# Two of sixteen head pairs of a hash attention: keys and queries grouped by two hash bits, products inside the four groups alone

## The chip, the cores and the metric

The kernel runs on one core of a Trainium2 chip. The metric is the device time of one execution in microseconds. Five engines work side by side, each through its own list of instructions in order: TensorE (PE; its weight loads are PEld), VectorE (DVE), ScalarE (ACT), GpSimd (POOL) and SyncE (SP), which does nothing but issue DMAs. An instruction that waits holds up everything behind it on its engine.

## The reference, cut to what matters

```python
batch, n_heads, seq, head_dim = (4, 8, 768, 64)
...
q_bits = (np.einsum('bhsd,dk->bhsk', q, proj) > 0)     # 6 bits
k_bits = (np.einsum('bhsd,dk->bhsk', k, proj) > 0)
...
mask = q_bucket[:, :, :, None] == k_bucket[:, :, None, :]
scores = np.where(mask, scale * np.matmul(q, k.transpose(0, 1, 3, 2)), -1e9)
...
attn = np.exp(scores - max)
out = np.matmul(attn / (attn.sum(-1) + 1e-9), v)
...
xt = x.transpose(0, 2, 1)                    # x: (B, S, 512), the heads side by side
u = x + (np.maximum(xt @ w_tok1, 0.0) @ w_tok2).transpose(0, 2, 1)
return u + np.maximum(u @ w_ch1, 0.0) @ w_ch2
```

A query sees only the keys whose six hash bits are all its own. What follows the attention is a token mixer (over the 768 positions) and a channel mixer (over the 512 channels).

## The kernel before

There are 32 heads of 768 tokens and 64 channels. Two heads of one batch are a **pair**, so there are 16 pairs, four to a batch, and the function `attention` walks through them in the loop over `n` at L560. A pair's 768 queries are two halves of 384; its 768 keys are six blocks of 128.

For each pair the loop does this, on engines that overlap from pair to pair:

- `scores` (L459): for each half and block a matmul of hash bits (bf16, L476) and two of channels (f32, L476 too) are summed in one pair of PSUM banks, so that a key of another bucket gets a large negative score. Each matmul uses 32 of the array's 128 rows, and four of them run side by side. ScalarE takes the exponential of each block (L388). PSUM has four pairs of banks, tag `sc`, handed out in turn, which scores, sums, hashes and weighted values all share.
- `Half.add` and `add_last` (L420, L430): VectorE sums the six blocks of exponentials of a half, five operations of 128x768 each half (L424, L428, L432).
- `Quotients.sums` (L503): TensorE sums over the keys with a matrix of ones (L509); ScalarE makes a first reciprocal as exp(-ln) (L513, L514); `newton` (L517) improves it on VectorE (L522, L524) and ScalarE spreads it (L530); `divide` (L532, L534) puts quotients into `XT`, the attention's result with channels on the partitions. The sums, `newton` and `divide` of a pair run during the pair after it.
- `Hash(n + 1)` (L317): TensorE projects the next pair's queries and keys (L325, L330), VectorE makes bits of them (L342, L343) into a scratch place in `XT`, and DMAs spread them to the rows of `bits` (`spread`, L335): eight from SP for keys (L350) and eight from POOL for queries (L353).
- `Half.weigh` (L434): TensorE multiplies exponentials and values (L443), ScalarE moves the result out (L453).
- `Conversion` (L133): the weights come as float64 and are turned to float32 in 12 chunks, one a pair in pairs 0 to 11: one ScalarE operation (L169), four on VectorE in `join` (L179 to L188) and one in `end` (L198).
- `bounce` (L220): after every second pair two pairs' results are transposed on VectorE in 32x32 blocks (L225) and written to DRAM (`bounced`, L230), from where `fetch` (L235, L237) brings a batch in token order into `x0` or `x1` for the mixer. The fetch of batch 0 into `x0` stands in pair 8.

After pair 15 the pools of the attention are given back, and the token mixer (L742 and L782) begins with batch 0, then the channel mixer (L869). The mixer's first matmul takes a PSUM bank that the attention's last `newton` has read.

All of it is written out by hand in the order in which each engine is to run it; no scheduler moves anything. DMAs of SP run through one queue in the order of issue. At its end the kernel looks whether any score was too large for the way in which exponentials are taken here (`excess`); if so a careful version runs everything again.

## Time and profile before

| | us |
|---|---|
| three runs | 780.22, 781.08, 781.44 (median 781.08) |
| the profiled execution | 779.55, its span 777.8 |
| attention in it, first scores to the mixer's first matmul | 5.84 to 301.93 |
| busy in the span: PE, PEld, DVE, ACT, POOL | 770.8, 513.0, 677.6, 453.5, 115.4 |

Times below are counted from the start of the span. A row of the chain of waits, in order of time, has the start, the length, and the engine, tile and line of a piece of the chain. A row of the timeline has the start, the time from the first to the last end of merged instructions, engine, line, operation, output and input with their shapes, and how many there are; in brackets stands how long the engine sat idle before it, and for whom. A row of groups has the busy time and the mean of one in ns behind the bar. A row of windows has the busy time of each engine in a stretch, the granted TensorE clock, the busy share of the DMA engines and GB/s.

### The profile page before, as it was taken

Reading aid. Unit: us, or ns where it says so; the run is one execution under the profiler, and the core shown is the slowest. Engines: PE = TensorE matmul, PEld = TensorE weight load, DVE = VectorE, ACT = ScalarE, POOL = GpSimd, SP = SyncE. Lnnn points to the kernel's source line nnn. Section 1 sums busy time; section 2 is a strip of 40 time slices with the busy share of each in tenths; the row PEclk is TensorE's granted clock in tenths of the full one; section 3 lists DMA queues with packets and bytes.
Section 4 is the critical chain, followed back from the end, with each engine's and each line's share of the span. In section 5 each row is a group of like instructions: output and inputs, shape, how many; then the busy total and the mean of one; then the engine's idle time right before and its main releaser. Section 6 shows DMA issues by size and latency. Waiting matters only on the chain.

```text
span 777.8 us, 14634 instructions
## 1 busy us (share of the span) xinstructions
PE 770.8 (99%) x5681; PEld 513.0 (66%) x5681; DVE 677.6 (87%) x935; ACT 453.5 (58%) x822; POOL 115.4 (15%) x195
## 2 busy tenths in 40 slices
PE   9999999999999999999999999999999999999997
PEld 4555655665666553555544458888877888886886
DVE  5999999999998787999697898999899799889884
ACT  6677777777777774433223235656675666675331
POOL 1222322222211110011121010210000131000001
PEclk9999999999999999999999999999999999999999
DMA  4435353547453324895686996897766685850665
GB/s 169 150 131 170 132 171 136 168 154 271 163 166 105 119 49 146 260 244 123 121 279 219 331 385 245 257 287 220 216 204 222 228 247 138 251 157 1 195 168 130
DMA packets 104314, 146.36 MB, mean 188 GB/s; under 512 B 32944, under 2 KB 76464, under 8 KB 102320
## 3 DMA queue, kind: packets, MB, share of 16 engines
q1 hardware_dynamic: 92384, 119.01, 46.2%
q0 software_dynamic: 11568, 26.13, 14.4%
q8 instruction: 46, 0.75, 0.4%
q10 hardware_dynamic: 288, 0.25, 0.1%
q14 instruction: 28, 0.23, 0.1%
HBM read 101.17 MB, written 35.52 MB: 176 GB/s over the span
## 4 chain that ended last, share of the span: by engine, by line
PE 97%; DVE 1%; ACT 1%; DMA 0%; issue 0%; DVEq 0%; SPq 0%
PE b L869 51%; PE sc L476 17%; PE acc L443 15%; PE t L742 5%; PE t L782 5%; PE hash L509 1%; PE sc L399 1%; PE hash L325 1%; PE hash L330 1%; ACT exps L388 0%; DMA qk<-in_qk 0%; DVE esd L432 0%; PE opening L362 0%; DVE esd L428 0%; ACT rec L530 0%
## 5 line engine op out<-in xcount | busy, mean ns | idle before, releaser
L388 ACT ACTIVATE exps<-sc 128x768 f32<-128x768 f32 (+1 forms) x207 | 144.6, 763 | 10.7 <-PE sc L476 7.6
L476 PE MATMUL sc<-qk 32*128 32x384 f32 (+1 forms) x1560 | 137.6, 458 | 0.0
L869 PE MATMUL b<-R,second 128*128 128x256 f32 (+1 forms) x522 | 131.8, 408 | 0.0
L443 PE MATMUL acc<-exps,vn 128*32 128x384 f32 (+1 forms) x1536 | 127.1, 486 | 0.0
L476 PEld LDWEIGHTS sc<-qk 32*128 32x128 f32 x1560 | 105.1, 185 | 21.7 <-issue 6.3
L869 PEld LDWEIGHTS b<-R,second 128*128 128x128 f32 x522 | 99.1, 190 | 28.5 <-issue 16.5
L443 PEld LDWEIGHTS acc<-exps,vn 128*32 128x32 f32 x1536 | 50.2, 109 | 70.8 <-issue 69.0
L353 POOL DMA_DIRECT2D bits<-XT x120 | 60.9, 509 | 216.1 <-issue 196.1
L875 ACT COPY c<-b 128x256 f32<-128x256 f32 (+1 forms) x96 | 40.3, 426 | 79.4 <-PE b L869 67.5
L428 DVE TENSOR_TENSOR esd<-esd,exps 128x768 f32<-128x768 f32 x64 | 61.3, 958 | 7.1 <-ACT exps L388 0.5
L432 DVE TENSOR_TENSOR esd<-esd,exps 128x768 f32<-128x768 f32 x64 | 61.3, 958 | 5.6
L530 ACT COPY rec<-rec 32x384 f32<-32x384 f32 x64 | 32.6, 510 | 55.0 <-DVE rec L524 53.4
L869 PE MATMUL b<-XT,WC 128*128 128x256 f32 (+1 forms) x208 | 61.0, 428 | 0.0
L476 PE MATMUL sc<-bits 32*128 32x384 bf16 (+1 forms) x390 | 54.8, 311 | 0.0
L869 PEld LDWEIGHTS b<-XT,WC 128*128 128x128 f32 x208 | 39.5, 190 | 15.4 <-issue 10.3
L869 PE MATMUL b<-XT,SW 128*128 128x256 f32 (+1 forms) x164 | 47.0, 410 | 0.0
L742 PE MATMUL t<-x,W 128*128 128x512 f32 x96 | 41.8, 593 | 0.4 <-DVE rec L522 0.4
L869 PEld LDWEIGHTS b<-XT,SW 128*128 128x128 f32 x164 | 31.1, 190 | 9.4 <-issue 4.1
L424 DVE SCALAR_TENSOR_TENSOR esd<-exps 128x768 f32<-128x768 f32 x32 | 30.3, 948 | 6.3 <-ACT exps L388 6.3
L742 PEld LDWEIGHTS t<-x,W 128*128 128x128 f32 x96 | 18.2, 190 | 23.1 <-issue 21.3
L1686 POOL DMA_DIRECT2D seen<-in_qk x21 | 12.6, 598 | 106.2 <-ACT seen L1676 70.3
L869 PE MATMUL b<-TA,WC 128*128 128x256 f32 (+1 forms) x84 | 28.2, 440 | 0.0
(253 smaller groups left out, 1314.5 us busy)
## 6 DMA issues: line engine op xcount, KB each, us to landing
qk<-in_qk_rows SPq DMA_DIRECT2D x15, 1152.0 KB
second<-left SPq DMA_DIRECT2D x20, 768.0 KB
raw<-in_moe_w_ch SPq DMA_DIRECT2D x16, 768.0 KB
second<-left SPq DMA_DIRECT2D x18, 576.0 KB
seen<-in_qk POOLq DMA_DIRECT2D x21, 384.0 KB, 4.6
WC<-hidden_left SPq DMA_DIRECT2D x18, 448.0 KB
vn<-in_v SPq DMA_DIRECT2D x16, 384.0 KB
x<-bounced SPq DMA_DIRECT2D x4, 1536.0 KB
```

Of the source, the lines that this page charges most:

```text
L353: nc.gpsimd.dma_start(out=to[at : at + 2 * BITS, half[j]], in_=g[of : of + 2 * BITS])
L388: return nc.scalar.activation(e[:, :, columns], sc, ACT.Exp, scale=SCALE)
L424: nc.vector.scalar_tensor_tensor(self.d, es[0], NR * EPS, es[1], op0=ALU.add, op1=ALU.add,)
L428: nc.vector.tensor_tensor(self.d, self.d, e, op=ALU.add)
L432: nc.vector.tensor_tensor(self.d, self.d, e, op=ALU.add)
L443: made = nc.tensor.matmul(acc[D * i + d : D * i + d + 32], vn[:, i, c, d : d + 32], e[:, i], start=(c == 0), stop=(c == NR - 1),)
L476: nc.tensor.matmul(made[j, piece][:, i], k[at : at + 32, ks], q[at : at + 32], start=part < 0, stop=part == 1,)
L530: nc.scalar.copy(rec[other : other + 32, h], rec[at : at + 32, h])
L742: nc.tensor.matmul(ps, W1[:, r, P * j : P * j + P], x[:, r], start=(r == 0), stop=(r == NR - 1),)
L782: nc.tensor.matmul(ps[at], left, right, start=start, stop=True, skip_group_check=True,)
L869: nc.tensor.matmul(ps, left(k), right(k), start=start and k == ks[0], stop=stop and k == ks[-1], skip_group_check=True,)
L875: nc.scalar.copy(c, ps)
```

## The change

Pairs 14 and 15 (batch 3, the last two) leave the loop, which now has `NREG` = 14 turns. Their tokens are put in order of two of the six hash bits, which makes four groups of at most 256 slots, and scores and values are computed inside the groups alone; the other four bits mask as before. The largest group that these inputs make in the two pairs has 235 tokens.

Each of the two is done in steps that hang at named points of the loop's turns (`at(n, point, ...)`):

- `prepare_sorting`, in turn 0: constants on POOL and VectorE, and four DMAs that fill the four tables in DRAM with zeros, 1024 rows each.
- `load` in the turn before `first`; in turn `first`: `hash`, `load_rows` (rows of tokens, three DMAs), `turn_bits`, `own_groups`, `count` (ranks by matmuls with triangles of ones); next turn `places` and `numbers`.
- `scatter`: 24 indirect DMAs of 128 rows on POOL, eight in each of three turns, write the rows to their slots.
- `fetch` in turn `made - 1`: 12 DMAs bring the slots back; `turn_q`, `copy_bits`, `turn_k`, `turn_sorted_bits` make operands of them.
- at the end of turn `made`, in one piece: `scores(0)`, `scores(1)`, `weigh`, then `divide` and `turn_back`, which also writes the results to DRAM.
- `gather`: 12 indirect DMAs on POOL in turns `back` and `back + 1`, then `store` (four DMAs) into `bounced[3]`.
- `fetch_turned` and `finish` in the last turn, 13: eight DMAs read both pairs' results back and VectorE transposes them into `XT`.

`first`, `made`, `back` are 1, 6, 9 for pair 14 and 5, 10, 11 for pair 15. The conversion of weights moves from turns 0 to 11 to turns 2 to 13, the fetch of batch 0 into `x0` from turn 8 to the end of turn 12, since `x0` now serves as scratch. The tile `rec` has one buffer in place of two, hash scratch lies elsewhere, and new inputs hold the two pairs' rows.

```diff
+    NG, SLOTS = 4, 256
+    QW, KW = D + 4, 2 * D + 4
+    SORTED = {B * NP - 2: (1, 6, 9), B * NP - 1: (5, 10, 11)}
+    NREG = B * NP - len(SORTED)
...
-                rec = self.rec = pool.tile([P, 2, HALF], F32, name="rec", tag="rec", bufs=2)
+                rec = self.rec = pool.tile([P, 2, HALF], F32, name="rec", tag="rec", bufs=1)
...
+        def prepare_sorting():
...
+            for tab in tables:
+                w = tab.shape[1]
+                nc.sync.dma_start(
+                    out=slots(tab).rearrange("(p j) c -> p j c", p=P),
+                    in_=nothing[:, :w].unsqueeze(1).broadcast_to((P, NJS, w)),
+                )
...
+            def load(self):
+                self.t = pool.tile([P, 2 * (S + HALF)], F32, name="qk", tag="qk", bufs=3)
+                nc.sync.dma_start(out=self.t, in_=sorted_qkv[self.which])
...
+            def hash(self):
...
+                for j in range(4):
+                    nc.tensor.matmul(
+                        ps[32 * j : 32 * j + 32], proj_apart, t[:, j % 2, half[j // 2]], start=True, stop=True,
+                    )
...
+            def count(self):
...
+                nc.scalar.copy(copy, self.ps[:, : at + 4])
...
+                for i in range(2):
+                    nc.scalar.copy(
+                        rows_kv[:, :, :, i, 2 * D : 2 * D + 4],
+                        bits[:, :, 1, i, :4].rearrange("p (a u) c -> p a u c", u=2),
+                    )
...
+            def scatter(self, count):
+                for r, w, i in self.todo[:count]:
...
+                    nc.gpsimd.indirect_dma_start(
+                        out=tables[2 * w + i],
+                        out_offset=bass.IndirectOffsetOnAxis(ap=self.at[:, x : x + 1], axis=0),
+                        in_=row, in_offset=None,
+                    )
...
+            def scores(self, k):
...
+                for i in range(2):
+                    for part in range(W + 1):
+                        for g in range(NG):
+                            rows = slice(32 * g, 32 * g + 32)
...
+                            nc.tensor.matmul(
+                                banks[g][:, SLOTS * i : SLOTS * i + SLOTS], left, right,
+                                start=part == 0, stop=part == W, skip_group_check=True,
+                            )
+                for g in range(NG):
+                    nc.scalar.activation(
+                        self.e[k][g], banks[g].rearrange("p (i s) -> p i s", i=2), ACT.Exp, scale=SCALE,
+                    )
+
+            def weigh(self):
...
+                for k in range(2):
+                    for g in range(NG):
+                        nc.tensor.matmul(
+                            ps[32 * g : 32 * g + 32], ones, self.e[k][g], start=k == 0, stop=k == 1,
+                            skip_group_check=True,
+                        )
...
+                    for i in range(2):
+                        for b in range(W):
+                            for g in range(NG):
+                                nc.tensor.matmul(
+                                    acc[32 * g : 32 * g + 32, i, SLOTS * b : SLOTS * b + SLOTS],
+                                    sorted_v[:, i, 2 * g + k, 32 * b : 32 * b + 32], self.e[k][g][:, i],
+                                    start=k == b == 0, stop=k == 1, skip_group_check=True,
+                                )
...
+        def fetch_turned():
+            stage = pool.tile([P, 2 * S], F32, name="stage", tag="stage", bufs=1)
+            for x, n in enumerate(SORTED):
...
+                for g in range(4):
+                    nc.sync.dma_start(out=y[32 * g : 32 * g + 32], in_=of[g, hp])
...
+        def finish():
+            for n, y in ys:
+                b, hp = pairs[n]
+                nc.vector.transpose(XT[:, hp, S * b : S * b + S].rearrange("p (a i) -> p a i", i=32), y)
...
+        at(0, "loads", prepare_sorting)
...
+            at(first - 1, "loads", call("load"))
+            at(first, "hash", call("hash"))
+            at(first, "loads", call("load_rows"))
+            at(first, "weighed", call("turn_bits"), call("own_groups"))
+            at(first, "end", call("count"))
+            at(first + 1, "begin", call("places"), call("numbers"))
+            for n in range(3):
+                at(first + 1 + n, "loads", call("scatter", 8))
+            at(made - 1, "added", call("fetch"))
+            at(made - 1, "last", call("turn_q"))
+            at(made, "begin", call("copy_bits"), call("turn_k"), call("turn_sorted_bits"))
+            at(made, "end", call("scores", 0), call("scores", 1), call("weigh"))
+            at(made, "last", call("divide"), call("turn_back"))
+            at(back, "loads", call("gather", range(4)))
+            at(back + 1, "begin", call("gather", range(4, NR)))
+            at(back + 1, "added", call("store"))
+        at(NREG - 1, "begin", fetch_turned)
+        at(NREG - 1, "added", finish)
+        at(NREG - 2, "last", lambda: fetch(0, x0))
...
-        for n in range(len(pairs)):
+        for n in range(NREG):
             halves = [Half(n, half) for half in range(2)]
+            converts = n >= NREG - weights_chunks
             if n:
                 load_v(n + 1)
+                now_at(n, "begin")
                 scores(halves)
                 hashing = bank_pair("hash")
                 halves[0].add()
                 halves[0].add_last()
+                now_at(n, "added")
...
-            if n == 2 * NP:
-                fetch(0, x0)
+            acc = bank_pair("acc")
+            now_at(n, "hash")
             halves[1].add_last()
...
             load_qk(n + 2)
-            weights.begin()
+            now_at(n, "loads")
+            if converts:
+                weights.begin()
...
             halves[1].weigh(acc)
+            now_at(n, "end")
             if n and n % 2 == 0:
                 bounce(pool.tile([P, 2 * S], F32, name="stage", tag="stage", bufs=1), n - 2)
+            now_at(n, "last")
```

Three places show what stands where now. The rows are the engine's instructions in their order, with the line in the kernel that each list belongs to (so `spread`'s L350 before is L373 in the change), the operation, the tile or tensor that is written and that which is read, and the shape; numbers behind a name are buffers.

**SyncE's queue, turns 0 and 1.** Before, from the load of pair 1's values to that of pair 3's queries and keys (`bits` is the hash bits, `raw` a chunk of weights):

```order
L283 DMA vn<-in_v 128x768
L265 DMA qk<-in_qk_rows 128x2304
L161 DMA raw<-in_moe_w_tok 128x3x512
L283 DMA vn<-in_v 128x768
L350 DMA bits_119<-XT 8x192 x8
L265 DMA qk<-in_qk_rows 128x2304
L161 DMA raw<-in_moe_w_tok 128x1536
```

In the change (`sorting` takes a projection, `table` are the four tables in DRAM, `in_sorted` pair 14's queries, keys and values):

```order
L296 DMA vn<-in_v 128x768
L278 DMA qk<-in_qk_rows 128x2304
L607 DMA sorting<-in_proj_pair 128x32
L653 DMA table_123<-x_110 1024x1x68
L653 DMA table_124<-x_110 1024x1x68
L653 DMA table_125<-x_110 1024x1x132
L653 DMA table_126<-x_110 1024x1x132
L673 DMA qk<-in_sorted 128x2304
L296 DMA vn<-in_v 128x768
L373 DMA bits_119<-XT 8x192 x8
L278 DMA qk<-in_qk_rows 128x2304
```

The four fills of the tables now stand ahead of pair 14's load, and the second and third chunk of weights are gone from here.

**SyncE's queue, turn 5.** Before, from the end of turn 4 to the end of turn 5:

```order
L230 DMA bounced_88<-stage 32x24x64 x4
L283 DMA vn<-in_v 128x768
L350 DMA bits_119<-XT 8x192 x8
L265 DMA qk<-in_qk_rows 128x2304
L161 DMA raw<-in_moe_w_ch 128x1536
```

In the change (`table` rows come back into `XT` and `WC`, `in_kv_rows` and `in_q_rows` are pair 15's rows of tokens):

```order
L296 DMA vn<-in_v 128x768
L804 DMA XT<-table_123 128x544
L804 DMA XT<-table_124 128x544
L810 DMA XT<-table_125 32x8x68 x4
L810 DMA XT<-table_126 32x8x68 x4
L812 DMA WC_85<-table_125 128x8x64
L812 DMA WC_85<-table_126 128x8x64
L373 DMA bits_119<-XT 8x192 x8
L278 DMA qk<-in_qk_rows 128x2304
L676 DMA XT<-in_kv_rows 128x3x528
L681 DMA XT<-in_q_rows 128x3x136
L681 DMA XT<-in_q_rows 128x408
```

The twelve DMAs of `fetch` stand ahead of the eight for the next pair's bits, and the three of `load_rows` behind the next load of queries and keys.

**SyncE's queue and VectorE's list, the end of attention.** SyncE before, from the values of pair 14 on (`bounced` is the result in DRAM, `x` a batch in token order):

```order
L283 DMA vn<-in_v 128x768
L350 DMA bits_119<-XT 8x192 x8
L265 DMA qk<-in_qk_rows 128x2304
L283 DMA vn<-in_v 128x768
L350 DMA bits_120<-XT 8x192 x8
L230 DMA bounced_91<-stage 32x24x64 x4
L237 DMA x_3736<-bounced_89 128x6x512
L161 DMA raw<-in_moe_w_ch 128x3x512 x2
```

In the change, from the values of pair 13 on (`stage` is both the source of `bounce` and the target of the last read back):

```order
L296 DMA vn<-in_v 128x768
L924 DMA bounced_91<-stage 128x6x32 x4
L373 DMA bits_120<-x_110 8x192 x8
L169 DMA raw<-in_moe_w_ch 128x1536
L238 DMA bounced_90<-stage 32x24x64 x4
L245 DMA x_110<-bounced_88 128x6x512
L935 DMA stage<-bounced_91 32x24x32 x8
L245 DMA x_3799<-bounced_89 128x6x512
```

`store`, then the bounce of pairs 10 and 11, the fetch of batch 0 and the eight reads of `fetch_turned` follow one another in the last two turns. VectorE before, the last pair:

```order
L432 TENSOR_TENSOR esd<-esd,exps 128x768 x2
L424 SCALAR_TENSOR_TENSOR esd<-exps 128x768
L428 TENSOR_TENSOR esd<-esd,exps 128x768 x2
L432 TENSOR_TENSOR esd<-esd,exps 128x768 x2
L522 TENSOR_TENSOR rec<-hash,near 128x384
L524 SCALAR_TENSOR_TENSOR rec<-rec,near 128x384 x2
L534 TENSOR_TENSOR XT<-num,rec 128x768
L522 TENSOR_TENSOR rec<-hash,near 128x384
L524 SCALAR_TENSOR_TENSOR rec<-rec,near 128x384 x2
L534 TENSOR_TENSOR XT<-num,rec 128x768
```

In the change, the last turn:

```order
L451 TENSOR_TENSOR esd<-esd,exps 128x768 x2
L455 TENSOR_TENSOR esd<-esd,exps 128x768 x2
L941 STREAM_TRANSPOSE XT<-stage 128x768 x2
L447 SCALAR_TENSOR_TENSOR esd<-exps 128x768
L451 TENSOR_TENSOR esd<-esd,exps 128x768 x2
L455 TENSOR_TENSOR esd<-esd,exps 128x768 x2
L545 TENSOR_TENSOR rec<-hash,near 128x384
L547 SCALAR_TENSOR_TENSOR rec<-rec,near 128x384 x2
L187 TENSOR_SCALAR unit<-size 128x768
L191 TENSOR_SCALAR size<-size 128x768
L195 SCALAR_TENSOR_TENSOR unit<-raw,unit 128x768
L196 TENSOR_TENSOR size<-size,unit 128x768
```

`finish` (L941) stands between the sums of the first and the second half, and four operations of a weight chunk (L187 to L196) between the two `newton`.

345 lines of the change are left out of this document (332 added, 13 removed).

## The prediction

> **What bounds the kernel now.** I read the chain of waits first, by engine and then in order of time, then VectorE's timeline, then the queues.
>
> ```profile
> PE 97%; DVE 1%; ACT 1%; DMA 0%; issue 0%; DVEq 0%; SPq 0%
> ```
> ```profile
> 136.24 9.16 PE sc L476 x104
> 145.41 0.78 PE hash L509 x8
> ...
> 146.82 7.76 PE acc L443 x96
> ...
> 154.59 9.16 PE sc L476 x102
> ...
> 283.14 3.04 PE sc L476 x38
> ...
> 301.93 20.87 PE t L742 x48
> 322.80 9.03 PE t L782 x28
> ```
> TensorE never waits: the chain runs from pair to pair on it alone. A pair takes 154.59 - 136.24 = 18.35 us: scores 9.16, sums 0.78, the next pair's hash about 0.6, values 7.76. The last pair's scores begin at 283.14 and the token mixer at 301.93, a tail of 18.79 us.
>
> ```profile
> 139.96 0.92 DVE L424 SCALAR_TENSOR_TENSOR esd<-exps 128x768 f32<-128x768 f32 x1
> ...
> 157.43 0.96 DVE L424 SCALAR_TENSOR_TENSOR esd<-exps 128x768 f32<-128x768 f32 x1
> ...
> 176.66 0.92 DVE L424 SCALAR_TENSOR_TENSOR esd<-exps 128x768 f32<-128x768 f32 x1
> ```
> These are VectorE's first sums of three pairs running. From the first to the second go 17.47 us, to the third 19.23 (a bounce, two transposes more): together 36.70, exactly two pairs of TensorE. In a pair with a weight chunk VectorE has no slack either.
>
> **The change, part by part.** Signs: plus is slower. The sum is made against the profiled execution, 779.55 us, which lies 1.5 below the median of 781.08.
>
> *Removed:* two pairs, 2 x 18.35 = **-36.7**. The edits of constants, of the hash's scratch place and the wider check of `excess` cost nothing: they lie beside TensorE's chain.
>
> *TensorE's work for a grouped pair.* An f32 matmul leaves two records in the trace (a pair's 48 for the values are the 96 of its row). Scores: 32 f32 and 16 bf16 matmuls of 256 columns stand where a pair has 48 and 24 of 384, two thirds of the matmuls with two thirds of the columns: 9.16 x 0.444 = 4.1 us; if a matmul costs the same whatever its width (48 for 78, as one block is cut in two), 5.6. Values: 32 of 256 for 48 of 384, 7.76 x 0.444 = 3.4, by count 5.2. Sums: 8 of 512 for 4 of 384, 2.1. Hash: 4 of 384, 0.8. Bits and ranks, 11 small ones, 0.6 (an estimate). That is 11.0 to 14.3.
>
> ```profile
> 120.96 7.33 ACT L388 ACTIVATE exps<-sc 128x768 f32<-128x768 f32 x10 [0.26 <-PE sc L476]
> ```
> Ten exponentials of 768 take 7.33, so eight of 512 take about 4.6, and the second half's end some 0.5 behind the point where TensorE could use them. I take 12 a pair: **+24** (22 to 29). VectorE's new work for such a pair (six transposes of 512, quotients, ranks, some 11 us) lies beside this piece; what spills into the neighbours I take as **+1** (0 to 3).
>
> [...] Here a record of an f32 matmul of 384 columns on all rows takes 9.03 / 28 = 0.32 us; the 96 records of a pair's f32 scores, one after another, would take 31.0, and with the bf16 ones they take 9.16, at least 3.4 times less. [...]
>
> *Pair 14's load, turn 1.*
>
> ```profile
> 1.40 0.29 POOL masks.py:199 TENSOR_SCALAR_AFFINE_SELECT ident<-ident 128x128 f32<-128x128 f32 x1
> ...
> 19.77 4.07 POOL L353 DMA_DIRECT2D bits<-XT  x8 [15.32 <-DVE XT L343]
> ```
> ```profile
> 24.66 0.42 SPq L265 DMA_DIRECT2D qk<-in_qk_rows  x1
> ```
> ```profile
> 36.22 0.16 PE hash L330
> ```
> ```profile
> 106.00:107.00 1.00, 1.00 (x18) 0.65 (x13) 0.90 (x2) 1.00 (x3) 0.00 (x0) 1.00 0.86 182
> ...
> 122.00:123.00 1.00, 1.00 (x18) 0.69 (x12) 0.90 (x2) 1.00 (x2) 0.00 (x0) 1.00 0.99 418
> ```
> POOL ends its bits at 23.8 and then has 22 small operations, at 0.2 each (the one at 1.40 is of the dearer kind) 4.5 us, before the tables can be filled: 28.3. The fills are 4 x 1024 pieces of 272 or 528 B, 1.64 MB. Bounce's pieces of 256 B move at 182 GB/s, long ones at 418 (the two windows); so 9 us, and then 1.18 MB of pair 14's load in 2.8 and about 1.5 to land: 41.5. TensorE is done with the next pair's hash at 36.4 and then stands before pair 14's: **+5** (0, if the queues overlap, to 9).
>
> *The indirect DMAs.* The trace shows none.
>
> ```profile
> L353 POOL DMA_DIRECT2D bits<-XT x120 | 60.9, 509 | 216.1 <-issue 196.1 <-DVE XT L343 15.3 <-DVE size L183 1.0
> ...
> L802 POOL DMA_DIRECT2D XT<-second x8 | 9.8, 1227 | 99.4 <-DMA x<-bounced 54.3 <-DVE second L801 22.0 <-DVE size L183 6.3
> ```
> ```profile
> bits<-XT POOLq DMA_DIRECT2D x120, 12.0 KB, 1.7
> ```
> A DMA of 16 rows costs POOL 0.51 us, one of 128 rows that adds 1.23. I take 1.2, nearest in rows; 0.5 to 2.5 (twice the dearer) are the ends. Landing takes 1.7.
>
> *Fetch and rows, turns 5 and 9.*
>
> ```profile
> 148.03 0.34 DVE L342 TENSOR_SCALAR XT<-hash 64x192 bf16<-64x192 f32 x1
> ...
> 154.75 0.96 DVE L188 TENSOR_TENSOR size<-size,unit 128x768 f32<-128x768 f32 x1
> ```
> ```profile
> 148.40 6.01 SPq L350 DMA_DIRECT2D bits<-XT  x8
> 154.45 0.44 SPq L265 DMA_DIRECT2D qk<-in_qk_rows  x1
> ```
> ```profile
> 149.54 4.41 POOL L353 DMA_DIRECT2D bits<-XT  x8 [14.36 <-issue]
> ```
> In the pair that begins at 136.24, SP issues key bits from 12.2 to 18.2 after its start and POOL ends its own at 17.7: they land just ahead of the next pair. Eight scatters behind POOL's bits end 27.3 after the start of turn 4 and land at 29.0, 10.6 into turn 5. Only then can SP issue the rest of `fetch`, until 15.1; the key bits behind it run to 21.1, the next load and `load_rows` to 23, and their 1.18 + 1.23 MB land at about 28.5. ScalarE's copies of bits into these rows wait for that, and behind them in its list are all exponentials of pair 6. TensorE gets there at 18.35 + 0.8 (hash) + 1.3 (`count` is reached at 18.35 and waits for `own_groups`, which stands behind VectorE's four chunk operations; the last ends 19.5 into the pair) + 0.6 = 21.0. Exponentials begin at 30 in place of 21.7; four banks of lead cover part. With the 1.3: **+8** (3 to 12). In turn 9 there are no rows; the first key bits land at 15.1 + 3 + 1.7 = 19.8, the later ones as late again: **+2** (0 to 6).
>
> *The end.*
>
> ```profile
> 117.89 9.16 PE sc L476 x104
> ```
> ```profile
> 138.20 1.83 DVE L225 STREAM_TRANSPOSE stage<-XT 128x768 f32<-128x768 f32 x2
> ```
> ```profile
> 140.06 3.65 SPq L230 DMA_DIRECT2D bounced<-stage  x4
> ```
> ```profile
> 285.98 0.96 DVE L424 SCALAR_TENSOR_TENSOR esd<-exps 128x768 f32<-128x768 f32 x1 [1.13 <-ACT exps L388]
> ...
> 291.12 0.95 DVE L424 SCALAR_TENSOR_TENSOR esd<-exps 128x768 f32<-128x768 f32 x1
> ...
> 296.24 0.55 DVE L522 TENSOR_TENSOR rec<-hash,near 128x384 f32<-128x384 f32 x1
> 296.82 1.15 DVE L524 SCALAR_TENSOR_TENSOR rec<-rec,near 128x384 f32<-128x384 f32 x2
> ...
> 301.32 0.56 DVE L522 TENSOR_TENSOR rec<-hash,near 128x384 f32<-128x384 f32 x1 [0.77 <-ACT near L514]
> ```
> Count from the start of turn 12. Twelve gathers of 1.2 behind turn 11's bits end at 13.8, land at 15.5, and `store` holds SP until 18.5. The key bits behind it land from 23.2 on: turn 13 begins 4.9 late. The bounce's DMAs, 22.2 after the start of their pair before (140.06 - 117.89, behind the transposes), go out from 24.9 and have landed at 31; they hold the tile `stage`, so the eight reads of `fetch_turned` are issued then, and they queue behind batch 0's 1.57 MB, which end at 34. 6,144 pieces of 128 B take 4.3 us at 182 GB/s by bytes, 8.6 if a piece costs what one of 256 B does; I take 7, landed at 42.7. VectorE reaches `finish` about 31 and stands there. Then: the second transpose 0.95; the second half's sums 296.24 - 291.12 = 5.12; from there to the mixer 301.93 - 296.24 = 5.69; the chunk's four operations and a quotient take 4.06 where 3.35 stood, +0.7. The mixer begins at 55.2, against 18.35 + 18.79 = 37.1: **+18** (12 to 24).
>
> *A cold TensorE.*
>
> ```profile
> 3.96 1.89 PE opening L362 x8
> ```
> ```profile
> 8.10 0.85 PE L362 MATMUL opening<-qk,projs 128*32 128x384 f32 x8
> ```
> The same eight matmuls take 1.89 us early on and 0.85 four us later. If 13 idle us bring that back, some 4 us run at 0.45 of the pace: **+2** (0 to 5). The granted clock stays at 1.00 in both stretches, so that column would not show it. [...]
>
> **Sum:** -36.7 + 24 + 1 + 5 + 8 + 2 + 18 + 2 = +23.3, so 802.9 of the profiled kind, 804 beside the median.
>
> **The rivals.**
>
> *Forecast: work leaves TensorE, waits for small DMAs take its place, most in the last turn.* 72%.
>
> *The pieces come in time.* Were pair 14's load, the rows, the bits and the read back all there when asked for, -36.7 + 24 + 1 + 1.3 and a tail of 2.6 (the two transposes and 0.7) would remain: -7.8, **773**. It decides at `finish`: the read back would have to land by 31 into turn 12 and 13. For it speaks that TensorE is the chain; against it that the reads may not even be issued before the bounce has landed. 11%.
>
> *Level.* All waits at their low ends: -36.7 + 22 + 3 + 12 = +0.3. 4%.
>
> *Indirect DMAs at 2.5.* Eight and the bits then need 24.1 us of POOL in turns of 18.35; six such turns push the query bits late by some 3 to 5 each, and the gathers add 13 to the end: about **835**. 13%.
>
> **Chances and range.** About 0.2% is what a measurement of this kernel tells from no change. Faster 11%, within 4%, slower 85%. The forecast's own bounds do not all meet at one end; 788 to 828 leaves out most of the first rival and the worse part of the last.
>
> **What would show it.** In the changed profile: turns without grouped work of 18.35; the grouped piece near 11 us; TensorE idle at the grouped hash in turn 1, on a DMA; ScalarE idle at the copies into `XT` between turns 5 and 6; VectorE idle some 10 us before `finish`, on the DMA of `stage`; POOL's indirect DMAs near 1.2. I am wrong if VectorE does not stand at `finish`, if the grouped piece needs 15, or if POOL's price moves the bits of every turn.

## The result, and the profile after

| | before | change |
|---|---|---|
| median of 4 runs each, us | 780.65 (779.26 to 781.44) | 835.61 (832.62 to 839.13) |
| ratio | 1 | 1.0708, 95% interval 1.0662 to 1.0754 |
| the profiled execution, its span, us | 779.55, 777.8 | 836.31, 834.6 |
| scores of turn 1 to the mixer's first matmul, us | 25.73 to 301.93 | 25.69 to 356.88 |

The change is slower, by more than twice what was forecast: 835.6 against 804, above the range's end of 828. Between the profiled executions lie 56.8 us, and 55.0 of them arise in the attention: the mixers begin 55.0 later and take 1.8 longer.

Before, TensorE was the chain of the attention up to the scores of the last pair. The first line of the chain of waits, by engine, now reads (shares of the whole span, attention and mixers; "issue" is time for which the profile shows no wait):

```profile
PE 53%; issue 20%; DVE 9%; DMA 8%; POOL 5%; SPq 4%; ACT 1%; DVEq 0%; POOLq 0%; ACTq 0%
```

The table below has the turns of the changed kernel, from the first matmul of a turn's scores to that of the next (in the last, to the mixer), and what each has beyond a turn's 18.35 us (the last: beyond 18.79).

| turn | 1 | 2 | 3, 4 | 5 | 6 | 7 | 8 | 9 | 10 | 11 | 12 | 13 |
|---|---|---|---|---|---|---|---|---|---|---|---|---|
| us | 36.23 | 18.98 | 18.35 | 40.90 | 28.77 | 18.66 | 19.07 | 24.15 | 30.92 | 18.66 | 24.43 | 33.72 |
| beyond | 17.9 | 0.6 | 0 | 22.6 | 10.4 | 0.3 | 0.7 | 5.8 | 12.6 | 0.3 | 6.1 | 14.9 |

Together 92 us, against 36.7 for the two pairs removed. Five places hold nearly all of it, and TensorE's timeline names a wait at each (the bracket is the idle time before the row and what ended it). The lines of the changed kernel are L690 for the grouped hash, L704 for `turn_bits`, L466 for values, L499 for scores, L532 for sums:

```profile
45.32 1.51 PE L690 MATMUL shash<-qk,sorting 128*32 128x384 f32 x8 [8.97 <-DMA bits<-XT]
46.57 5.77 PE L466 MATMUL acc<-exps,vn 128*32 128x385 f32 x48
55.52 0.23 PE L704 MATMUL shash<-sorting,XT 128*128 128x40 bf16 x3 [3.18 <-DMA XT<-in_q_rows]
55.67 5.78 PE L466 MATMUL acc<-exps,vn 128*32 128x384 f32 x48
...
128.07 0.82 PE L690 MATMUL shash<-qk,sorting 128*32 128x384 f32 x8
128.72 4.06 PE L466 MATMUL acc<-exps,vn 128*32 128x385 f32 x48
151.99 0.26 PE L704 MATMUL shash<-sorting,XT 128*128 128x40 bf16 x3 [19.21 <-DMA XT<-in_q_rows]
152.18 5.84 PE L466 MATMUL acc<-exps,vn 128*32 128x384 f32 x48
...
249.15 0.95 PE L499 MATMUL sc<-bits 32*128 32x192 bf16 x4 [5.30 <-DMA bits<-XT]
...
323.16 0.98 PE L499 MATMUL sc<-bits 32*128 32x192 bf16 x4 [5.78 <-DMA bits<-x]
...
334.84 4.07 PE L466 MATMUL acc<-exps,vn 128*32 128x385 f32 x48
350.76 1.51 PE L532 MATMUL hash<-esd,ones 128*32 128x384 f32 x8 [11.86 <-DVE rec L545]
352.04 4.91 PE L466 MATMUL acc<-exps,vn 128*32 128x384 f32 x48
```

Turn 1 stands twice, 8.97 and 3.18 us (the first bracket names key bits, whose DMAs were going out at the time; load_first below shows that the wait was for pair 14's load); turn 5 once, 19.21 us in the middle of its values; turns 10 and 13 begin 5.30 and 5.78 late for key or query bits; in turn 13 the sums wait 11.86 for VectorE. These are 54.3 us of idle time. The rest is work and pace. The grouped products of pair 14 stand in the chain, in order of time, between these two rows:

```profile
177.74 4.01 PE ss L851 x80
...
187.34 1.63 PE sc L499 x22
```

From the first (grouped scores) to the last (the next turn's) go 9.6 us. The pace shows in the rows above: the same eight matmuls L690 take 1.51 us behind an idle stretch and 0.82 without, half a pair's values 5.77, 5.84 and 4.91 in place of 4.06. The windows around the first stall have TensorE's busy time as their third number and the granted clock behind the five engines:

```profile
36.00:38.00 2.00, 0.35 (x10) 0.00 (x0) 1.72 (x3) 1.05 (x3) 0.00 (x0) 1.00 1.30 125
38.00:40.00 2.00, 0.00 (x0) 0.00 (x0) 0.00 (x0) 0.00 (x0) 1.92 (x4) 0.94 1.24 185
40.00:42.00 2.00, 0.00 (x0) 0.00 (x0) 0.00 (x0) 0.00 (x0) 1.77 (x5) 0.50 1.05 322
...
48.00:50.00 2.00, 2.00 (x20) 0.76 (x16) 1.86 (x4) 0.00 (x0) 0.00 (x0) 0.50 0.84 276
50.00:52.00 2.00, 2.00 (x31) 0.69 (x22) 1.08 (x2) 1.35 (x3) 0.00 (x0) 1.00 0.95 364
```

TensorE's work ends 0.35 us behind 36; the granted clock falls to 0.50 shortly before 40, 3.4 us later, and is back at 50, 4.7 us after work began again at 45.32. So this column does show it. Read in short windows, it does so at all six idle stretches listed above: the clock falls 2.2 to 4.6 us after TensorE's last matmul and is back 3.0 to 5.7 us after the next, so neither is a fixed delay.

Where the 19.21 us of turn 5 come from is read on SyncE's queue (a row is a run of DMAs being issued; L804 to L812 are `fetch`, L373 the key bits of the next turn, L676 and L681 the rows of tokens) and on POOL's groups:

```profile
129.60 1.96 SPq L804 DMA_DIRECT2D XT<-table  x2
133.01 3.77 SPq L810 DMA_DIRECT2D XT<-table  x8
136.83 1.08 SPq L812 DMA_DIRECT2D WC<-table  x2
138.01 5.50 SPq L373 DMA_DIRECT2D bits<-XT  x8
143.60 0.38 SPq L278 DMA_DIRECT2D qk<-in_qk_rows  x1
144.21 0.64 SPq L676 DMA_DIRECT2D XT<-in_kv_rows  x1
144.95 1.38 SPq L681 DMA_DIRECT2D XT<-in_q_rows  x2
```
```profile
L793 POOL DMA_INDIRECT table<-XT,sorting x48 | 59.2, 1234 | 23.0 <-issue 11.3 <-DMA table<-XT,sorting 8.0 <-ACT exps L411 2.6
...
L914 POOL DMA_INDIRECT stage<-result,sorting x24 | 27.7, 1153 | 7.9 <-issue 5.8 <-DMA bits<-XT 0.8 <-DMA stage<-result,sorting 0.6
```

The order is the predicted one. `fetch` waits for the last scatter (the second row starts 3.4 us behind the first), the key bits stand behind it, and the rows behind both; they are issued at 144.2 to 146.3 and have landed at 151.9. An indirect DMA costs POOL 1.23 us, as taken, but 0.30 lie between two, and the fifth of eight waits for an earlier one to land: eight take 13.1 us (79.75 to 92.81 in turn 2), 1.63 each.

At the end VectorE waits for the read back at `finish` (L941):

```profile
331.11 2.02 DVE L455 TENSOR_TENSOR esd<-esd,exps 128x768 f32<-128x768 f32 x2
341.77 0.98 DVE L941 STREAM_TRANSPOSE XT<-stage 128x768 f32<-128x768 f32 x1 [8.64 <-DMA stage<-bounced]
344.17 0.98 DVE L941 STREAM_TRANSPOSE XT<-stage 128x768 f32<-128x768 f32 x1 [1.42 <-DMA stage<-bounced]
```

It stands 10.1 us between the sums of the two halves, and TensorE 11.86 for the `newton` that follows.

### The profile page after: what moved, and what is told of

The parts are those of the page before. It is cut to its first block, busy times and chain, and to the rows that moved or that the text cites. A ratio compares the mean times of both kernels' runs of the same rounds, so it can differ in the third digit from the quotient of the medians.

```text
span 834.6 us, 14593 instructions
## 1 busy us (share of the span) xinstructions
PE 771.8 (92%) x5549; PEld 517.1 (62%) x5549; DVE 674.9 (81%) x965; ACT 445.4 (53%) x828; POOL 198.0 (24%) x274
## 4 chain that ended last, share of the span: by engine, by line
PE 53%; issue 20%; DVE 9%; DMA 8%; POOL 5%; SPq 4%; ACT 1%; DVEq 0%; POOLq 0%; ACTq 0%
PE b L1319 25%; PE acc L466 7%; PE sc L499 7%; PE t L1192 5%; PE t L1232 4%; DVE esd L451 2%; DVE esd L455 2%; DMA XT<-in_q_rows 2%; POOL table L793 1%; DMA bits<-XT 1%; SPq L373 1%; DMA seen<-in_qk 1%; POOL bits L376 1%; PE sc L422 1%; POOL seen L2136 1%
## 5 line engine op out<-in xcount | busy, mean ns | idle before, releaser
L411 ACT ACTIVATE exps<-sc 128x768 f32<-128x768 f32 (+1 forms) x181 | 126.2, 765 | 22.2 <-PE sc L499 20.2
L499 PE MATMUL sc<-qk 32*128 32x384 f32 (+1 forms) x1352 | 125.8, 470 | 0.0
L466 PE MATMUL acc<-exps,vn 128*32 128x385 f32 (+1 forms) x1344 | 117.7, 506 | 0.0
L499 PEld LDWEIGHTS sc<-qk 32*128 32x128 f32 x1352 | 97.1, 192 | 15.5 <-issue 3.8
L466 PEld LDWEIGHTS acc<-exps,vn 128*32 128x32 f32 x1344 | 45.4, 113 | 67.1 <-issue 66.0
L376 POOL DMA_DIRECT2D bits<-XT x96 | 49.8, 523 | 141.4 <-DVE XT L366 76.3
L793 POOL DMA_INDIRECT table<-XT,sorting x48 | 59.2, 1234 | 23.0 <-issue 11.3
L499 PE MATMUL sc<-bits 32*128 32x384 bf16 (+1 forms) x338 | 51.6, 317 | 11.2 <-DMA bits<-x 5.8
L553 ACT COPY rec<-rec 32x384 f32<-32x384 f32 x56 | 28.5, 510 | 60.2 <-DVE rec L547 58.7
L451 DVE TENSOR_TENSOR esd<-esd,exps 128x768 f32<-128x768 f32 x56 | 53.7, 960 | 7.0 <-ACT exps L411 1.2
L455 DVE TENSOR_TENSOR esd<-esd,exps 128x768 f32<-128x768 f32 x56 | 53.7, 959 | 5.2 <-DVE esd L455 0.5
L2136 POOL DMA_DIRECT2D seen<-in_qk x21 | 13.1, 624 | 108.4 <-ACT seen L2126 72.4
L1252 POOL DMA_DIRECT2D XT<-second x8 | 9.8, 1230 | 114.3 <-DMA x<-bounced 68.9
L2029 POOL DMA_DIRECT2D out<-second x7 | 8.7, 1238 | 112.6 <-ACT TB L1325 73.8
```

Source lines behind the costliest of these rows:

```text
L376: nc.gpsimd.dma_start(out=to[at : at + 2 * BITS, half[j]], in_=g[of : of + 2 * BITS])
L411: return nc.scalar.activation(e[:, :, columns], sc, ACT.Exp, scale=SCALE)
L451: nc.vector.tensor_tensor(self.d, self.d, e, op=ALU.add)
L455: nc.vector.tensor_tensor(self.d, self.d, e, op=ALU.add)
L466: made = nc.tensor.matmul(acc[D * i + d : D * i + d + 32], vn[:, i, c, d : d + 32], e[:, i], start=(c == 0), stop=(c == NR - 1),)
L499: nc.tensor.matmul(made[j, piece][:, i], k[at : at + 32, ks], q[at : at + 32], start=part < 0, stop=part == 1,)
```

## The experiments

Eighteen runs, in sets that shared a chip. The unaltered change ran again in two of them and gave 836.9 and 838.4. Lengths of turns are of the profiled execution.

| set | run | median us | ratio to before, 95% interval |
|---|---|---|---|
| chip 8 | load_first | 851.0 | 1.0886 to 1.0925 |
| | bits_apart | 843.9 | 1.0793 to 1.0844 |
| | made7 | 847.2 | 1.0840 to 1.0928 |
| | finish_late | 838.7 | 1.0741 to 1.0780 |
| chip 10 | change_again | 836.9 | 1.0699 to 1.0752 |
| | store_finish | 821.8 | 1.0495 to 1.0548 |
| | fetch_late | 835.0 | 1.0649 to 1.0740 |
| | all_six | 807.4 | 1.0302 to 1.0364 |
| chip 7 | bits_copies | 839.3 | 1.0737 to 1.0770 |
| | rows_free | 828.1 | 1.0603 to 1.0636 |
| | best | 806.2 | 1.0306 to 1.0350 |
| | best_chunks | 805.8 | 1.0318 to 1.0362 |
| chip 10 | change_third | 838.4 | 1.0701 to 1.0749 |
| | no_gathers | 832.5 | 1.0632 to 1.0671 |
| | best2 | 804.2 | 1.0282 to 1.0311 |
| | best2_chunks | 810.2 | 1.0369 to 1.0398 |
| chip 15 | best3 | 776.4 | 0.9931 to 0.9958 |
| chip 5 | rows_back | 812.8 | 1.0388 to 1.0453 |

### One edit each

**load_first** swaps the table fills and pair 14's load; `fill_tables` is the loop of fills, taken out of `prepare_sorting`, and stands behind `load` now:

```diff
-            for tab in tables:
+        def fill_tables():
+            nothing = flat(x0)[:, 1024 : 1024 + KW]
+            for tab in tables:
...
+        at(0, "loads", fill_tables)
```

> Pair 14's load stands ahead of the four fills of the tables in SP's queue, in turn 0; nothing else is changed. If the stall of turn 1 is the load queued behind the fills, TensorE's 9.0 us before the grouped hash go, and with them the half clock that follows the idle stretch (granted clock 0.50 from 40 to 50): turn 1 falls from 36.2 us to 22 to 24, the run to about 822. Rival: the fills take the DMA engines for their 10 us wherever they stand, so that key bits and rows come as late as before: turn 1 stays over 30, the run over 830.

```profile
38.39 0.85 PE L693 MATMUL shash<-qk,sorting 128*32 128x384 f32 x8 [1.66 <-DMA qk<-in_sorted]
...
56.24 0.26 PE L707 MATMUL shash<-sorting,XT 128*128 128x40 bf16 x3 [13.12 <-DMA XT<-in_q_rows]
```

TensorE's timeline of this run: the load is nearly in time (1.66 us in place of 9 to 11), but the rows of tokens come no earlier than in the change (the wait for them ends 30.2 us into the turn, there 29.8), and TensorE now stands for them for 13.12. Turn 1 takes 37.7 us where finish_late, with turn 1 as in the change, has 36.0. The load was the first wait and hid a second; the rival holds.

**bits_apart** takes the grouped hash's bits out of `XT`:

```diff
-                self.bits = XT[:, self.which, at : at + HALF // 2].bitcast(BF16)
+                self.bits = self.t[:, : HALF // 2].bitcast(BF16)
```

> The grouped hash's bits are put into the tile of queries and keys (free by then) and no longer into XT, where the rows of tokens land too, in other columns. If turn_bits waits for the rows only because both are in one tile, TensorE goes on at about 133 in turn 5 (in place of 152) and without the 3.2 us in turn 1; ScalarE's copies of bits into the rows then still stand until the rows have landed (152), so exponentials of turn 6 begin near 154 in place of 160.6: about 6 gained in turn 5 and 2 in turn 1, the run at 828. Rival 1: the wait at turn_bits is for something that it needs: 835. Rival 2: the rows' landing holds nobody else: 19 + 3 gained, 813.

In this run TensorE passes `turn_bits` in turn 5 without a stop, and stands later, in the scores of turn 6; ScalarE's timeline shows for whom (L738 are the copies into the rows):

```profile
153.38 0.50 PE L499 MATMUL sc<-bits 32*128 32x384 bf16 x2 [8.30 <-ACT exps L411]
```
```profile
151.12 0.33 ACT L738 COPY XT<-sorting 128x24 f32<-128x24 f32 x2 [11.28 <-DMA XT<-in_kv_rows]
```

So nothing that `turn_bits` needs was late in the change. The DMAs of the rows write other columns of `XT`, in three planes at once; TensorE's wait stood in its list because bits and rows share a tile. This is the step that the prediction missed, and it is a wait of the program, not of the data. Without it turns 5 and 6 take 64.2 us in place of finish_late's 72.0, and turn 1 33.7 in place of 36.0: 10 gained, 8 expected.

**made7** makes pair 14's products one turn later, so that turn 5 has no fetch ahead of the rows:

```diff
-    SORTED = {B * NP - 2: (1, 6, 9), B * NP - 1: (5, 10, 11)}
+    SORTED = {B * NP - 2: (1, 7, 9), B * NP - 1: (5, 10, 11)}
```

> Pair 14's fetch and products are one turn later (made 7 in place of 6), so that in turn 5 pair 15's rows are queued behind the key bits alone and not behind the twelve DMAs of fetch. If that queue makes the rows late, they land near 143 in place of 151.9, and turn 5 falls from 40.9 to about 32: the run at 826; turn 6, with the fetch, then gets some 5 late by its key bits, so 826 to 831. Rival: the rows wait for the last scatter of turn 4 (landed at 133) and their own transfer, and the fetch adds little: less than 3 gained.

```profile
145.23 0.26 PE L704 MATMUL shash<-sorting,XT 128*128 128x40 bf16 x3 [10.92 <-DMA XT<-in_q_rows]
```

TensorE idles 10.92 us at `turn_bits` where finish_late has 17.96: the fetch in the queue was 7 of the 18. Turn 5 falls from 41.7 to 32.6 us as expected, but turn 8, next to the later products, rises from 19.3 to 23.4 and turn 9 from 22.5 to 24.3: part of it is given back.

**finish_late** puts `finish` behind the attention's last quotient:

```diff
-        at(NREG - 1, "added", finish)
...
         before.divide()
+        finish()
```

> finish (the last two transposes, from the read back) stands behind the attention's last quotient on VectorE in place of between the two halves' sums of the last turn. If VectorE's 10.1 us of idle time at finish hold the end up, the sums of the second half begin at about 333 in place of 345, and the mixer at 345 in place of 357: the run at 823. Rival: something else is late then, the second half's values or the batch 0 in token order: the mixer begins at 350 or later, the run at 828 or more.

The last turn takes 20.3 us; the three others of the set, with `finish` in its place, have 33.6 to 35.4. That is 13 to 15 gained where 12 were expected: VectorE at `finish` was the end's price, and nothing took its place.

The medians of this set cannot be compared with 835.6: in all four turn 10 takes 38.6 to 40.2 us, not 30.9. finish_late and the 13 us it gains would make the unaltered change 852 here. TensorE's weight loads (PEld) of finish_late in turn 10 beside POOL's gathers show what is different:

```profile
264.22 0.20 PEld L499 LDWEIGHTS sc<-qk 32*128 32x128 f32 x2 [1.22 <-issue]
265.63 0.28 PEld L499 LDWEIGHTS sc<-qk 32*128 32x128 f32 x1 [1.22 <-issue]
```
```profile
263.45 0.95 POOL L914 DMA_INDIRECT stage<-result,sorting  x1 [0.30 <-issue]
264.71 0.95 POOL L914 DMA_INDIRECT stage<-result,sorting  x1 [0.30 <-issue]
```

TensorE's list advances in steps of up to 1.2 us, put down to no wait ("issue"), at the gathers' pace and up to their end. In rows_free, with the same steps on chip 7, the granted clock reads 0.54 from 240 to 244 us and 0.60 from 244 to 248. The steps stood in turn 10 on chips 8, 7 and 5 in all nine kernels run there, and on chip 10 in none of eight (seven with gathers), the unaltered change twice among them, nor in the first trace or on chip 15. It goes with the chip, as far as these runs go; the unaltered change was not run on chips 5, 7 or 8, and what holds TensorE there stays open. Below, only runs of one chip, or turns free of it, are compared.

### The last turns and the fetch

**change_again** is the change unaltered.

> The change itself, unaltered, so that it and the edits share a chip and a set of runs. The four edits before gave 839 to 851 where single stalls shrank as named; if that is the chip's or the run's doing, the unaltered change is at 848 to 855 here, and its turn 10 takes 38 to 40 us as in those four, not 30.9. If the edits themselves cost it, it is at 835 again.

836.9 us, turn 10 of 30.8 us.

**store_finish** is finish_late with `store` behind the key bits:

```diff
-            at(back + 1, "added", call("store"))
+            at(back + 1, "loads", call("store"))
```

> finish behind the last quotient, as before, and store (four DMAs) behind the key bits in SP's queue, not ahead of them, in turns 10 and 12. If store holds the key bits of turn 13 up, turn 12 falls from 24.4 to 18.7 us, and with finish at its end nothing takes its place: 6 less than finish_late, 19 less than change_again. Rival: the end waits for the read back, which then comes 3 us later: no more than 2 less than finish_late.

15 us less than change_again. Turn 12 falls from 24.3 to 22.2 only: the key bits are in time, but POOL's query bits, behind twelve gathers, are not, and turn 13 still begins 3.5 late.

**fetch_late** puts `fetch` behind the key bits and moves the transposes and copies of what it brings:

```diff
-            at(made - 1, "added", call("fetch"))
-            at(made - 1, "last", call("turn_q"))
-            at(made, "begin", call("copy_bits"), call("turn_k"), call("turn_sorted_bits"))
+            at(made - 1, "loads", call("fetch"))
+            at(made, "added", call("copy_bits"), call("turn_q"), call("turn_k"), call("turn_sorted_bits"))
```

> The twelve DMAs of fetch stand behind the next pair's key bits, and the transposes and copies of what they bring behind the sums of the first half in the turn after. If fetch, which waits for the last scatter, holds the key bits up in turn 9, turn 9 falls from 24 to 19 us and turn 10 is not cold at its start: some 8 less. In turn 5 the rows still stand behind fetch, so that it stays at 40. Rival: POOL's own query bits come as late (behind eight scatters), and turn 9 stays above 22.

Turn 9 falls from 23.5 to 18.5 us as expected, so the key bits behind `fetch` were its wait. But turn 10 rises from 30.8 to 33.5, since VectorE now has 4.0 us of transposes between the sums of the halves and waits 2.2 us there for what they turn, its `newton` is late, and the grouped scores wait 3.75 us for a bank that ScalarE empties after it. 1.9 us remain of 8, and the runs of the two overlap (830.8 to 837.2 against 836.0 to 838.5).

**all_six** is all six edits.

> All six edits: load ahead of the fills, bits in the tile of queries and keys, made 7, finish at the end, store and fetch behind the key bits. If the stalls named so far are all there is, turn 1 is near 24, turn 5 near 30, turns 6, 9 and 12 near 19, the last turn near 20: 36.7 less, some 21 of TensorE's work for two grouped pairs more, and 20 to 25 of stalls: 785 to 792. Rival: POOL and its queue set the pace of turns 2 to 12 (18.1 us of bits and indirect DMAs each), and each stall only moves to the next: over 805.

807.4: 29.6 less than change_again, but 15 to 22 above what was expected, and the rival's bound is met though not for its reason. Turns 3, 4, 8 and 9, full of bits and indirect DMAs, take 18.3 to 18.7 us, so POOL sets no pace. What is left are the next waits in line: turn 2 idles 6.8 and turn 6 4.8 us for ScalarE, which stands at its copies for the rows.

**no_gathers** leaves the 24 gathers out; **change_third** beside it is the unaltered change.

```diff
-                        nc.gpsimd.indirect_dma_start(
-                            out=self.x[:, r, i], out_offset=None, in_=self.results[i],
...
+                        nc.gpsimd.memset(self.x[:, r, i], 0.0)
```

> The 24 gathers are left out and their tile filled with zeros (the last two pairs' results are missing), all else as in the change. If the gathers hold up the last turns (POOL's key and query bits and store behind them) turn 12 falls from 24.4 to 18.7 and the read back starts 10 earlier, so that finish waits less: the last turn falls from 33.7 to 25 or less; 836 to 822. If the gaps in TensorE's list come from the gathers, they are gone too where change_third has them. Rival: store and the bounce, not the gathers, make the end late: over 830.

> The change itself, unaltered, again as the measure for this set. In two of three sets so far the kernels with edits showed gaps of about 1.2 us in TensorE's own list in turn 10 that the trace puts down to no wait, in steps of POOL's gathers (turn 10 then takes 38 to 40 us in place of 30). If that goes with the chip, the unaltered change shows it here exactly when the edits beside it do; if it goes with the edits, the change has turn 10 at 30.8 and the edits at 37 or more.

Turn 12 falls from 24.5 to 18.6 us, the gathers' whole share. The last turn grows, from 34.0 to 36.0: the read back ends 4.4 earlier (VectorE's last transpose at 341.9 in place of 346.4), turn 13 begins 5.7 earlier, and TensorE idles 15.40 for `finish` in place of 12.21. 832.5 where 822 was expected; the rival's bound holds. That the bounce and the read back behind it set the end is read from the order in SyncE's queue, where the reads start at 329.3 in place of 334.8, behind the bounce in both; no run takes the bounce away. change_third has no gaps in turn 10 (31.0), nor has any other run of its set, which leaves the gathers' part in the gaps untested.

### Towards a version without the waits

**bits_copies** is bits_apart with ScalarE's copies into the rows taken out of `count` and put a turn later:

```diff
+            def complete_rows(self):
                 bits = copy[:, :BW].rearrange("p (r w i c) -> p r w i c", w=2, i=2, c=CW)
...
+            at(first + 1, "added", call("complete_rows"))
```

> The bits in the tile of queries and keys, and ScalarE's copies of bits into the rows behind the exponentials of the turn after, so that nobody stands for the rows before their scatter; all else as in the change. If the rows of tokens are what turn 5 waits for, TensorE no longer idles there at turn_bits: turn 5 falls from 40.9 to about 20, turn 6 then begins with its key bits (queued behind fetch) some 8 late: turns 5 and 6 together from 69.7 to 57, turn 1 from 36.2 to 31; 836 to 818. Rival: the rows only pass the wait on to the scatters and from there to turn 9, which grows by as much: over 828.

Turns 5 and 6 take 64.3 us, as in bits_apart. ScalarE shows why (L818 is `copy_bits`, which brings fetched bits of pair 14 from `XT`):

```profile
147.78 0.24 ACT L818 CAST x<-XT 128x64 bf16<-128x64 f32 x1 [11.17 <-DMA XT<-in_kv_rows]
```

`copy_bits` reads neither the rows nor their columns, yet waits for their DMAs: the same shared tile, once more, at the next instruction. The forecast of 13 fails, and the rival with it, for turn 9 is not longer.

**rows_free** adds the fills ahead of the first turn:

```diff
         before = None
+        fill_tables()
         for n in range(NREG):
```

> As bits_copies, and the four fills of the tables go out before the first turn, where the DMA engines carry next to nothing (12 to 26 us). If turn 1 was the fills ahead of pair 14's load, and the rows behind both, turn 1 falls to 20 to 21 and no half clock follows: 10 less than bits_copies, 808. Rival: something else is late in turn 1, the key bits that the fills now push, or the first weights: less than 4 gained.

Turn 1 falls from 32.9 to 19.8 us, and the run by 11.2: the one long wait that bits_copies still had in turn 1, 10.81 us for the load, was the fills. The wait for the rows was gone from that turn already, so this run says nothing of it; rows_back below does.

**best** is rows_free with made 7, `finish`, `store` and `fetch` late, and the second gathers behind the query bits; **best_chunks** besides has no weight chunk in turns 7 and 10 (the last two lines):

```diff
-            at(back + 1, "begin", call("gather", range(4, NR)))
+            at(back + 1, "loads", call("gather", range(4, NR)))
-            at(back + 1, "added", call("store"))
+            at(back + 1, "end", call("store"))
...
-            converts = n >= NREG - weights_chunks
+            converts = n not in [it[1] for it in SORTED.values()]
```

> rows_free with pair 14 made in turn 7, fetch and its transposes late, the second gathers and store behind the next pair's bits, finish at the end. If the named waits are the whole of the loss, turns 1 and 5 take 20 each, 7 and 10 30 to 32 (VectorE is late by the transposes), 12 near 19, 13 near 19.5: 19 less than rows_free in the rest, about 778 to 785, level with the kernel before. Rival: bits and indirect DMAs fill POOL to 18.1 us a turn and hold query bits back: over 795.

> best with the twelve weight chunks in the turns 0 to 13 but 7 and 10, so that VectorE has no chunk in the two turns with products of a grouped pair. If VectorE's 17.5 us a turn with a chunk hold the grouped products up (TensorE then waits for a bank that ScalarE empties late), turns 7 and 10 fall to about 28.5: 3 to 6 less than best, 773 to 780, and so faster than the kernel before. Rival: the chunks in turns 0 and 1 cost as much there: as best.

806.2 and 805.8, above what was expected by 20 and more, some of it the chip's gaps (turn 10 37.7 us). VectorE's timeline of best shows what the edit made:

```profile
256.30 1.84 DVE L233 STREAM_TRANSPOSE stage<-XT 128x768 f32<-128x768 f32 x2 [9.79 <-DMA bounced<-stage]
...
307.32 1.84 DVE L233 STREAM_TRANSPOSE stage<-XT 128x768 f32<-128x768 f32 x2 [7.23 <-DMA bounced<-stage]
```

The bounce's transposes write `stage`, which the gathers and the late `store` now hold longest, and VectorE stands 9.79 and 7.23 us. Chunks elsewhere gain nothing on the whole: in the profiled executions (805.5 and 810.3 us) turns 1 and 2 lose 5.8 us by them, and turn 11 wins 5.9.

**best2** gathers in one turn; **best2_chunks** is that without chunks in turns 7 and 10. The expectation speaks of four gathers ahead of the query bits and eight behind; the kernel had eight ahead and four behind.

```diff
+            at(back, "begin", call("gather", range(4)))
+            at(back, "loads", call("gather", range(4, NR)))
+            at(back + 1, "loads", call("store"))
```

> best, but the gathers stand in one turn, the first four ahead of that turn's query bits and eight behind them, and store behind the key bits of the turn after. In best the bounce's transposes on VectorE stood 9.8 and 7.2 us for the late store, which holds the same tile. If that was what best lost, turns 11 and 13 fall from 25.3 and 28.2 to about 19.5 each: 15 less than best, 785 to 792 (less by 8 more on a chip without the gaps). Rival: query bits get late behind the gathers in the turn itself, and the time only moves: over 800.

> best2 with the weight chunks kept out of the two turns with grouped products. If VectorE's chunk holds these products up, turns 7 and 10 are 3 shorter each: 780 to 787 and level with the kernel before. Rival: as best2, as best_chunks was as best.

804.2 and 810.2. The last turn is 21.4 us, but turns 10 and 12 begin 12.84 and 9.16 us late, for bits behind the gathers: the rival holds. In turn 9 the gathers stand behind the last eight scatters (191.1 to 205.2); in turn 11 none starts before 265.4, behind the DMAs of the bounce and of pair 15's results (issued from 256.1 to 261.9). Chunks elsewhere cost 6.

**best3** gives pair 15's gathers a place of their own and VectorE's transposes a later one, behind `newton`:

```diff
+                    if self.which:
+                        stage = flat(x0)[:, 4 * W * SLOTS :]
...
+            if it.which:
+                at(back, "begin", call("gather", range(2)))
+                at(back, "loads", call("gather", range(2, NR)))
+            else:
+                at(back, "loads", call("gather", range(4)))
+                at(back + 1, "begin", call("gather", range(4, NR)))
...
+            at(made, "newton", call("turn_q"), call("turn_k"), call("turn_sorted_bits"))
```

> best2 with three things changed: pair 15's gathers go into the scratch of x0, which is free by then, and not into stage, four of them ahead of turn 11's query bits and eight behind; pair 14's gathers as in the change; the transposes for grouped products stand on VectorE behind newton, not between the sums of the two halves. If what best2 still loses are the named waits (bits behind the gathers 12.8 and 9.2, a bank that ScalarE empties late 2.7 and 1.7), turns 7 and 10 take about 30, turns 9, 11 and 12 about 19, turn 13 about 20: the mixer begins near 296 to 300, the run at 773 to 780, and the change is worth some us. Rival: VectorE or POOL has no room left and the waits move once more: 785 or more.

776.35 us (775.74 to 777.11, 5 runs) against 780.91 (779.78 to 781.62, 9 runs): 0.6% faster than the kernel before. Its turns:

| turn | 1 | 2 to 4 | 5 | 6 | 7 | 8 | 9 | 10 | 11 | 12 | 13 |
|---|---|---|---|---|---|---|---|---|---|---|---|
| us | 19.85 | 18.35 | 21.04 | 18.35 | 29.96 | 18.66 | 18.35 | 30.53 | 18.66 | 19.88 | 19.02 |

TensorE is busy for 759 of 774 us, and the mean granted clock is 1.0, where the change's is 0.963. The largest wait left on it from turn 1 on is for the transposes of what `fetch` brought:

```profile
160.35 4.09 PE L854 MATMUL ss<-x 32*128 32x256 bf16 x80 [1.95 <-DVE x L839]
```

The mixer begins at 295.1, 6.9 earlier than before; 3.1 of these are lost again in the mixers, which no run looked into.

**rows_back** is best3 with one edit undone, which has two parts: the bits are in `XT` again, and so are the copies at the turn's end.

> best3 with one of its edits undone: the bits of the grouped hash are in XT again and ScalarE's copies into the rows stand again at the end of the turn, as in the change. If the wait for the rows at turn_bits is a loss of its own and not a mere shadow of late fetches, TensorE idles some 6 to 12 us in the middle of turns 1 and 5 with all else in time, and a half clock follows each: turn 1 from 19.9 to 30, turn 5 from 20 to 31, 776 to 797 to 802. Rival: with the rows issued early the wait is short: under 785.

```profile
50.38 0.26 PE L706 MATMUL shash<-sorting,XT 128*128 128x40 bf16 x3 [9.64 <-DMA XT<-in_q_rows]
50.56 6.97 PE L466 MATMUL acc<-exps,vn 128*32 128x384 f32 x48
...
140.39 0.26 PE L706 MATMUL shash<-sorting,XT 128*128 128x40 bf16 x3 [10.57 <-DMA XT<-in_q_rows]
140.58 6.34 PE L466 MATMUL acc<-exps,vn 128*32 128x384 f32 x48
```

With everything else in time TensorE idles 9.64 and 10.57 us at `turn_bits`, and half a pair's values behind it takes 6.97 and 6.34 in place of 4.06. Turn 1 is 32.5 us in place of 19.9, turns 5 and 6 together 51.5 in place of 39.4: 24.7 for two waits that no data asks for. In turn 1 the fills are long out of the way here, and the rows still come late. The rest of the 36 us between the two runs is chip 5's gaps (turn 10 39.0) and turns 2, 3 and 8; the forecast of 797 to 802 left these out.

## Why the prediction was wrong

| term | forecast | measured | from |
|---|---|---|---|
| pairs removed | -36.7 | -36.7 | turns 3 and 4, 18.35 |
| TensorE's work | +24 | +22 | two pieces of 9.6, two hashes and counts of some 1.4 |
| turn 1 | +5 | +12.2 | idle 8.97 and 3.18 |
| turn 5 to 6 | +8 | +19.2 | idle 19.21 |
| turn 9 to 10 | +2 | +5.8 | turn 9, 24.15 |
| the end | +18 | +18 | turn 12, 6.1, and the idle 11.9 of turn 13 |
| half clock | +2 | +12 | turn 1 4.0, turn 5 1.9, turn 10 2.8, turn 13 3.2 |
| VectorE, mixers | +1 | +4.5 | turns 2, 6, 7, 8, 11 and 1.8 in the mixers |

The measured column adds up to 57.0, for the 56.8 between the profiled executions. The half clock's row is an estimate: half of TensorE's busy time while the granted clock read 0.50 (the eight matmuls L690 took 1.51 us there and 0.82 at 1.00). Of the 33.5 us that the forecast lacked, 11 are turns 5 and 6, 10 the half clock, 7 turn 1 and 4 turn 9.

- **Right:** the pairs' 18.35, and a grouped pair's TensorE work, which came to some 11 where the low bound said 11.0 and 12 was taken; the exponentials, with which the 12 was argued, in fact lie beside. Turns without grouped work stay at 18.35 to 19.07. `finish` stands for the read back as described: turn 13 began 5.8 late (4.9 said), the read back had landed 45.4 after the start of turn 12 (42.7 said), and the mixer began at 58.2 (55.2 said), the 3.2 of half clock in turn 13 among them. finish_late shows that `finish` decides. An indirect DMA costs 1.23 us (1.2 taken).
- **The step that failed** is the one on turn 5. It reads: "ScalarE's copies of bits into these rows wait for that, and behind them in its list are all exponentials of pair 6", with "four banks of lead" to cover part. The rows did come late, for the reasons given: they landed 34 us into the turn, where about 28.5 was said, some 4 of it because eight scatters take 13.3 (117.5 to 130.8) and not 9.6. But TensorE did not get as far as the scores. It stood by itself, halfway through the values, at a 0.26 us matmul whose operand lies in the same tile as the rows. bits_apart took that wait away and found the predicted one behind it, 8.30 us long; rows_back put it back, in turns 1 and 5, into a kernel in which all else is in time, and it cost 24.7 in the two. The prediction put nothing on it. In turn 1 of the change the same wait is the second idle stretch, only 3.18 because the load had already held TensorE up.
- **A mechanism that was right, sized too small:** the half clock. It was forecast for one place, the end, at +2. It followed all six stops, of 3.18 us and more; TensorE was busy for 23.8 us at a granted clock of 0.50, so some 12 were lost, by the estimate above. That it would not show in the granted clock was wrong: it reads 0.50.
- **Sizes, turn 1:** the DMA engines moved 125 to 185 GB/s from 32 to 40 us, while the fills ran, and the load landed at 45 where 41.5 was said (the 1.5 to land in that were an estimate, beside the 1.7 of POOL's bits); the rows behind it were not thought of. load_first and rows_free show the first wait to be the fills. The second is not theirs alone: rows_back has the fills ahead of turn 1, and TensorE stands 9.64 us at the same place.
- **Sizes, turn 9:** +2 taken, 3 to 4 below the truth. The key bits' DMAs start at 244.6, because `fetch` waits for the last scatter to land; fetch_late shows this wait, and with it 5.0 us, to be real.
- **The rivals:** the one that gave 835 came out by its number and not by its mechanism. An indirect DMA does not cost 2.5, and POOL's bits are not late in every turn: turns 3 and 4 lose nothing, turn 7 0.3. "Level" asked for all waits at their low ends, and none was there. "The pieces come in time", at 773 and 11%, is what best3 comes near: the same grouped work with its waits removed is 4.6 us faster than the kernel before, on one chip. The change's idea was worth a little; its places in five lists cost some sixty (835.6 against 776.4 us).

## What to carry to other kernels

Work that was moved off the bounding engine brought waits onto it here, 54.3 us in six stops; look first at the short instructions that the new work puts into that engine's own list, at what each of them waits for, and whether that is its data or only a neighbour in the same tile. In the change a stop of TensorE cost more than its length: a stretch at a granted clock of 0.50 followed each of the six, of 3.18 to 19.21 us, and cost some 2 us more, an estimate from the 12 above. Taking one wait away mostly shows the next: here single edits gained 0 to 15 us, and only the version with none of the named ones left was faster than the start.
